# Quadrant scores and fp32 half-column values in the attention of a fused attention and rational MoE kernel

## Chip, cores, metric

The program runs on one core of one Trainium2 chip. The metric is device time in microseconds (us); before the change the median of three runs is 899.58 us (899.51 to 901.82). Below, the engines are called PE (TensorE, the matrix engine), PEld (its weight loads), DVE (VectorE), ACT (ScalarE), POOL (GpSimd) and SP (SyncE, which here only issues DMAs).

## What is computed

Attention over 8 batches, 8 heads, 576 tokens, head size 64, with keys and values averaged over runs of 8 tokens (72 remain), and then on the 4608 x 512 result a two-layer product with a rational function between the layers:

```python
    k_p = k.reshape(B, H, Sp, pool, D).mean(axis=3)
    v_p = v.reshape(B, H, Sp, pool, D).mean(axis=3)
    scores = scale * np.matmul(q, k_p.transpose(0, 1, 3, 2))
    scores = scores - np.max(scores, axis=-1, keepdims=True)
    attn = np.exp(scores)
    attn = attn / (np.sum(attn, axis=-1, keepdims=True) + 1e-09)
    return np.matmul(attn, v_p).astype(np.float32)
...
    h = x @ w_in
    h2 = h * h
    h3 = h2 * h
    P = a[0] + a[1] * h + a[2] * h2 + a[3] * h3
    Q = 1.0 + np.abs(b[0]) * np.abs(h) + np.abs(b[1]) * h2
    g = P / (Q + 1e-06)
    return (g @ w_out).astype(np.float32)
```

## The kernel before

**Blocks and units.** The 4608 tokens are cut into 18 blocks of 256. For a block, `attend` makes the attention output x, transposed (512 features in 4 groups of 128 partitions). Then 8 units of 256 hidden features follow: `mm1` makes `ph` (24 products of 256 columns), `rational` turns it into `gh` and `gl` on ACT, DVE and POOL, and `mm2` adds 12 products of 512 columns to the two sums `po`. The operands of these products are of type fp32r. What must be finer than one such operand is written as a sum of two parts (x as x0 + x1, g as gh + gl, each weight as two), and three products of parts are added. The units of blocks 0 and 1 run in two halves, those of 2 and 3 beside each other; from block 4 on, blocks follow one another.

**Attention of a block.** It has two tiles of 128 tokens. `attention` transposes q (on PE for blocks 0 to 3, on DVE after that), and makes the scores `ps` in fp32: pairs of heads lie on 128 partitions, the pooled keys `kpT` of a pair stand in a block-diagonal 128 x 144 operand whose other half is zero, so one product makes two heads' scores of 128 tokens. Then DVE takes the maximum and subtracts it, ACT does exp, DVE sums, and POOL multiplies by the reciprocal. The 144 probabilities of a pair of heads are more than 128 partitions hold, so 128 (`main`) and 16 (`rem`, `REM = 16`) go separate ways. They are transposed with DVE's 32 x 32 blocks and 16 DMAs a block into `lo` (the buffer am1; on PE for blocks 0 to 3), and then ACT and DVE split them into the parts `hi` and `lo` (am0 and am1). `values` makes four products for each pair of heads: values' high part by `hi`, low part by `hi`, the remainders (`vr`), and high part by `lo`.

**Block and batch limits do not coincide.** A batch has 576 tokens, 4.5 tiles. Four score tiles (4, 13, 22 and 31, in blocks 2, 6, 11 and 15) hold two batches and run each product as two of 64 tokens; six blocks (2, 4, 6, 11, 13 and 15) hold two batches in `values`, with twice as many products of fewer columns.

**Preparation.** `prep_k` and `prep_v` pool keys and values of a batch and `split_v` masks and splits the values. For batch 0 and 1, `prep_v_early` sums the runs on PE by products with the identity (`pvs`, `pvr`), with data in weight tiles that are free at that time.

**What sets the order.** `Plan` gives every instruction a cost, a due time and its buffers, lays them out on the engines, and issues them engine by engine in that order; at run time each engine goes through its list and waits on semaphores. `FAST`, `PACE` and `SLOW` set the due times. Where the plan sees PE without work, `issue` (lines 279 to 316) puts in filler products: `idle` before the first unit, and later products of the tile `zero` added to a sum `po`. All instructions that go through the plan have line 314 in the profile, fillers have 305; they are told apart by tile names: `ps` scores, `pv` values, `pm` and `pr` transposed probabilities, `pq` transposed q, `pk` and `pl` transposed keys, `am` the probabilities on partitions, `st_v` staged values, `e` the probabilities, `vm` and `vr` the split values.

## Time and profile before

| what | value |
|---|---|
| runs | 899.58, 899.51, 901.82 us |
| the profiled execution | 900.71 us, its span 899.0 us |
| PE busy | 883.1 us (98%) |
| DVE, ACT, POOL busy | 771.7, 679.1, 524.5 us |
| bytes moved | 75.33 MB, a mean of 84 GB/s |
| granted PE clock, mean | 0.998 of full speed |

The span is the time from the first to the last instruction. A matmul's record is longer than the time until the next one starts, since they are pipelined: rates are read from the starts of successive groups in the timeline, not from durations.

### The profile page before, as it was taken

The numbers are of one execution on the slowest core, as the hardware profiler recorded it, in microseconds if no ns is written. First come the engines' busy times: TensorE is split into PE (matmuls) and PEld (weight loads), VectorE is DVE, ScalarE is ACT, GpSimd is POOL, SyncE is SP. The second block draws the span as 40 slices with busy tenths as digits, with TensorE's granted clock in tenths as the row PEclk, the third lists the DMA queues.
The fourth block names the chain that finished last, engine by engine and source line by source line (L and its number), as shares of the span: only waits on it lengthen the run. The fifth ranks groups of instructions, "written<-read, shape, count | busy, mean of one in ns | idle before, by whom it ended". The sixth has DMA issues, their size and how long they took to land.

```text
span 899.0 us, 17101 instructions
## 1 busy us (share of the span) xinstructions
PE 883.1 (98%) x6158; PEld 824.7 (92%) x6158; DVE 771.7 (86%) x1335; ACT 679.1 (76%) x1126; POOL 524.5 (58%) x474
## 2 busy tenths in 40 slices
PE   7999999999999999999999999999999999999998
PEld 7898899899998999999999999999999999999997
DVE  6989988899979889987999798979897988788764
ACT  3998888878677777778677778686868787768765
POOL 4787687776546645354745485546644755445443
PEclk9999999999999999999999999999999999999999
DMA  9996110154243403031622252224412421202000
GB/s 267 315 379 232 25 54 1 47 147 124 69 91 72 129 16 70 16 73 26 137 45 45 58 132 58 37 46 89 112 32 58 94 60 25 60 1 61 1 24 24
DMA packets 185073, 75.33 MB, mean 84 GB/s; under 512 B 162332, under 2 KB 162332, under 8 KB 184988
## 3 DMA queue, kind: packets, MB, share of 16 engines
q1 hardware_dynamic: 184988, 74.23, 32.3%
q8 instruction: 49, 0.80, 0.4%
q14 instruction: 36, 0.29, 0.1%
HBM read 50.59 MB, written 12.58 MB: 70 GB/s over the span
## 4 chain that ended last, share of the span: by engine, by line
PE 70%; DVE 13%; ACT 6%; POOL 4%; SPq 2%; DMA 2%; issue 2%; ACTq 0%; POOLq 0%; DVEq 0%
PE ph L314 32%; PE po L314 30%; DVE t L314 4%; PE pv L314 3%; PE ps L314 3%; SPq L314 2%; ACT rp L314 2%; DVE rp L314 1%; DMA q<-in_q_dram 1%; POOL gl L314 1%; DVE sm L314 1%; POOL wout L314 1%; DVE m_win L314 1%; POOL w L314 1%; DVE am L314 1%
## 5 line engine op out<-in xcount | busy, mean ns | idle before, releaser
L314 PEld LDWEIGHTS ph<-x,win 128*128 128x128 f32 x3264 | 475.2, 191 | 42.0 <-DVE t L314 1.9
L314 PE MATMUL ph<-x,win 128*128 128x256 f32 x3264 | 488.0, 276 | 1.9 <-DVE t L314 1.1
L314 PE MATMUL po<-wout,gh 128*128 128x512 f32 x1152 | 342.8, 383 | 1.9 <-DVE am L314 1.2
L314 POOL TENSOR_TENSOR w<-w,r 128x512 f32<-128x512 f32 (+1 forms) x145 | 191.5, 1321 | 220.2 <-ACT r L314 210.9
L314 POOL TENSOR_TENSOR gl<-t,gh 128x512 fp32r<-128x512 f32 (+1 forms) x145 | 189.4, 1307 | 75.6 <-ACT gh L314 74.9
L314 PEld LDWEIGHTS po<-wout,gh 128*128 128x128 f32 x1152 | 179.8, 192 | 7.7 <-DVE am L314 1.6
L314 PE MATMUL po<-wout,gl 128*128 128x512 f32 x576 | 173.5, 383 | 0.0
L314 ACT ACTIVATE t<-ph,abn 128x512 f32<-128x512 f32 (+1 forms) x145 | 111.9, 772 | 58.2 <-PE ph L314 28.3
L314 DVE SCALAR_TENSOR_TENSOR t<-t,abn,rp 128x512 f32<-128x512 f32 (+1 forms) x145 | 109.0, 752 | 35.7 <-ACT rp L314 34.3
L314 DVE TENSOR_TENSOR t<-t,ph 128x512 f32<-128x512 f32 (+1 forms) x145 | 97.8, 678 | 40.6 <-ACT t L314 36.6
L314 ACT ACTIVATE r<-w,abn 128x512 f32<-128x512 f32 (+1 forms) x145 | 117.5, 811 | 16.6 <-POOL gl L314 6.1
L314 ACT CAST gh<-t 128x512 fp32r<-128x512 f32 (+1 forms) x145 | 88.5, 611 | 32.6 <-DVE t L314 32.4
L314 DVE SCALAR_TENSOR_TENSOR t<-t,abn,ph 128x512 f32<-128x512 f32 (+1 forms) x145 | 106.8, 738 | 2.6
L314 ACT ACTIVATE rp<-w 128x512 f32<-128x512 f32 (+1 forms) x145 | 86.5, 596 | 27.9 <-POOL w L314 20.7
L314 DVE SCALAR_TENSOR_TENSOR t<-rp,t 128x512 f32<-128x512 f32 (+1 forms) x145 | 98.9, 683 | 2.4
L314 ACT ACTIVATE w<-ph 128x512 f32<-128x512 f32 (+1 forms) x145 | 85.7, 592 | 20.1 <-DVE t L314 13.0
L314 DVE SCALAR_TENSOR_TENSOR rp<-w,rp 128x512 f32<-128x512 f32 (+1 forms) x145 | 99.4, 685 | 0.4
L314 PEld LDWEIGHTS po<-wout,gl 128*128 128x128 f32 x576 | 89.1, 192 | 1.4 <-POOL gl L314 0.2
L314 ACT ACTIVATE rp<-rp 128x512 f32<-128x512 f32 (+1 forms) x145 | 84.2, 581 | 2.6
L314 POOL TENSOR_TENSOR e<-e,sm 128x576 f32<-128x576 f32 x36 | 42.1, 1186 | 42.7 <-DVE sm L314 34.6
L314 PE MATMUL pv<-am,vm 128*128 128x256 f32 (+3 forms) x288 | 44.3, 275 | 0.6 <-DVE t L314 0.6
L314 PEld LDWEIGHTS pv<-am,vm 128*128 128x128 f32 x288 | 41.9, 191 | 1.9 <-DVE t L314 1.0
(109 smaller groups left out, 860.1 us busy)
## 6 DMA issues: line engine op xcount, KB each, us to landing
am<-e SPq DMA_DIRECT2D x224, 48.0 KB, 2.2
out_dram<-ob SPq DMA_DIRECT2D x17, 512.0 KB, 3.1
rwin<-in_moe_w_in_dram SPq DMA_DIRECT2D x8, 1024.0 KB, 9.6
rwout<-in_moe_w_out_dram SPq DMA_DIRECT2D x8, 1024.0 KB, 11.3
st_k<-in_k_dram SPq DMA_DIRECT2D x12, 512.0 KB, 5.0
st_v<-in_v_dram SPq DMA_DIRECT2D x12, 512.0 KB, 3.9
q<-in_q_dram SPq DMA_DIRECT2D x144, 32.0 KB, 2.0
st_v<-in_v_dram SPq DMA_DIRECT2D x48, 64.0 KB, 2.2
```

The source lines that it names most:

```text
L314: getattr(engines[op.eng], name)(*map(value, args), **{k: value(v) for k, v in kw.items()})
```

## The change

Scores: `kpT` is no longer block diagonal. Each head of a pair keeps its 64 feature rows in its own half of the partitions, and `quarters` makes each product as four of 64 x 64: two halves of the rows (the two heads) and two halves of the columns (tokens 0 to 63 and 64 to 127 of the tile), each with 72 columns streamed. The two heads write to two PSUM banks. Every tile has 16 such products, whether or not two batches meet in it.

Probabilities: each head's 72 go to 72 partitions of one buffer `am`, in fp32, without a split in parts. From block 4 on, DVE transposes 64 of the 72 in one instruction and the last 32 into a new tile `er` in another, and 12 DMAs a block (instead of 16) place them. For blocks 0 to 3 PE makes 8 transposes a tile instead of 6 and ACT and DVE copy them (`turn`).

Values: they stay whole in fp32 in `vp`, 72 partitions; `split_v`, the masks and the zeroing of `kpT` are gone. `values` makes one product per head, 72 x 64 by 256 columns, two heads of a pair in the two column halves, and both halves of the block in one step of the plan (but for block 0). `prep_v` runs POOL sums for 4 pairs of heads instead of 3 sets, `prep_v_early` runs all sums of 8 on PE. The pool `rat` has 6 buffers instead of 5.

```diff
-    pool("rat", 5)
+    pool("rat", 6)
...
-    kpT = [new("cpool", f"kpT{i}", [P, NJ, 2 * SP], F32, f"kpT{i}") for i in range(2)]
-    vm = [[new("cpool", f"vm{s}{i}", [P, NJ, P], F32R, f"vm{s}{i}") for s in range(2)]
-          for i in range(2)]
-    vr = [new("cpool", f"vr{i}", [P, NJ, D], F32R, f"vr{i}") for i in range(2)]
+    kpT = [new("cpool", f"kpT{i}", [P, NJ, SP], F32, f"kpT{i}") for i in range(2)]
+    vp = [new("cpool", f"vp{i}", [P, H, D], F32, f"vp{i}") for i in range(2)]
...
+    def prep_v_early(n, c):
+
         if n == 0:
-            for c in range(2):
-                js = slice(2 * c, 2 * c + 2)
-                half = early(0, 2)[:, c * CW:(c + 1) * CW].rearrange("p (j x) -> p j x", j=2)
-                dma(512, half, rows[js, REM:, :].rearrange("j r x -> r j x"))
-                dve(RW, port=True).tensor_tensor(
-                    out=half[:, :, 0:RW // 2], in0=half[:, :, 0:RW // 2],
-                    in1=half[:, :, RW // 2:RW], op=ALU.add)
-                for t in range(0, G // 2, 2):
-                    pe(430, [mm(vs[:, js], ident, half[:, :, s * D:(s + 1) * D], s == 0,
-                                s == G // 2 - 1) for s in range(t, t + 2)], claims=(vs,))
...
-            dma(1024, st, rows[:, REM:, :].rearrange("j r x -> r j x"))
-            st = st.rearrange("p j (t d) -> p t j d", t=G)
-            for t in range(0, G, 2):
-                pe(863, [mm(vs, ident, st[:, s], s == 0, s == G - 1)
-                         for s in range(t, t + 2)], claims=(vs,))
-        place = early(n, 1)
...
-        split_v(n, vs, vrs, False)
+            homes = [(early(m, 1)[:, CW:2 * CW], 2 * (1 - m), 2) for m in (1, 0)]
+        for place, h0, nh in homes:
+            st = place[:SP].rearrange("p (h x) -> p h x", h=nh)
+            dma(2 * SP * nh, st, v_place(n, 4 * c + h0, nh))
+            vs = bank(f"pvs{n}_{4 * c + h0}", [P, nh, D])[:SP]
+            step = G if n else 2
+            for t in range(0, G, step):
+                pe(109 * nh * step, [mm(vs, ident[:SP, :SP], st[:, :, s * D:(s + 1) * D],
+                                     s == 0, s == G - 1) for s in range(t, t + step)], claims=(vs,))
+            act(nh * D).copy(vp[n % 2][:SP, 4 * c + h0:4 * c + h0 + nh, :], vs)
...
+        for h in range(0, H, 2):
+            place = new("stage", "st", [P, 1024], F32, f"st_v{n}_{h}")[:SP]
+            st = place.rearrange("p (h x) -> p h x", h=2)
+            dma(4 * SP, st, v_place(n, h, 2))
...
-            while w > D:
-                gp(2 * w).tensor_tensor(out=st[:, :, 0:w], in0=st[:, :, 0:w],
-                                        in1=st[:, :, w:2 * w], op=ALU.add)
+            while w >= D:
+                to = st[:, :, 0:w] if w > D else vp[n % 2][:SP, h:h + 2, :]
...
-    def attention(t, hi, lo, qs, es):
+    def quarters(banks, j0, js, q, sg, at=0):
+
+        return [mm(banks[hh][r0:r1, at + j - j0, :], q[hh * D:(hh + 1) * D, j, r0:r1],
+                   kpT[n % 2][hh * D:(hh + 1) * D, j, :], True, True)
+                for j in js for a0, a1, n in sg for r0 in range(a0, a1, D)
+                for r1 in (r0 + D,) for hh in range(2)]
...
-        scores = [bank(f"ps{t}_{c}", [P, 4, SP]) for c in range(2)]
-        calls = [mm(scores[c][r0:r1, 2 * jj:2 * jj + 2, :], qT[:, 2 * c + jj, r0:r1],
-                    kpT[n % 2][:, 2 * c + jj, :], True, True)
-                 for c in range(2) for jj in range(2) for r0, r1, n in sg]
-        for part in [calls] if len(sg) > 1 else [calls[:2], calls[2:]]:
-            pe(1350 if len(sg) > 1 else 244 * 2, part, claims=(e, mx, sm))
-        for c in range(2):
-            hs = slice(4 * c, 4 * c + 4)
-            js = slice(2 * c, 2 * c + 2)
...
+        scores = [bank(f"ps{t}_{hh}", [P, NJ, SP]) for hh in range(2)]
+        pe(754, quarters(scores, 0, range(NJ), qT, sg), claims=(e, mx, sm))
+        for hh in range(2):
+            dve(NJ * SP).tensor_reduce(out=mx[:, hh, :], in_=scores[hh], op=ALU.max, axis=AX.X)
+            dve(NJ * SP).tensor_tensor(
+                out=es[:, hh:H:2, m, :], in0=scores[hh],
+                in1=mx[:, hh, :].unsqueeze(2).to_broadcast([P, NJ, SP]), op=ALU.subtract)
...
+        gp(450).tensor_tensor(out=e, in0=e, in1=sm.unsqueeze(2).to_broadcast([P, H, SP]),
+                              op=ALU.mult)
         if t >= 2 * SQ:
+            dve(H * HB).transpose(er[:, :, m, :], es[:, :, m, SP - HB:])
+            main = es[:, :, m, 0:2 * HB].rearrange("p h (g s) -> p h g s", s=HB)
+            dve(2 * H * HB).transpose(main, main)
+        else:
             for c in range(2):
-                dve(P).transpose(four[c], rem[c])
-            squares = main.rearrange("p j (g s) -> p j g s", s=HB)
-            dve(NJ * P).transpose(squares, squares)
+                turn(f"pm{t}_{c}", [es[:, h, m, :] for h in range(4 * c, 4 * c + 4)],
+                     am[:SP, 8 * c + m:8 * c + 8:2, :], c, am)
+
+    def turn(name, rows, to, c, am):
+
+        pm = bank(name, [P, 4, P])[:SP]
+        pe(110 * 4, [("transpose", (pm[:, x, :], row, ident), {}) for x, row in enumerate(rows)],
...
+        if c == 0:
+            act(4 * P).copy(to, pm)
...
-            pm = bank(f"pm{t}", [P, NJ, P])
-            pe(110 * NJ, [("transpose", (pm[:, j, :], main[:, j], ident), {})
-                          for j in range(NJ)], claims=(hi, lo))
-            act(NJ * P).copy(hi[:, :, col], pm)
-            dve(NJ * P).tensor_tensor(
-                out=lo[:, 0:NJ, col], in0=pm, in1=hi[:, :, col].bitcast(F32), op=ALU.subtract)
-            for c in range(2):
-                act(P).copy(four[c], rem[c])
-            pr = bank(f"pr{t}", [P, 2, P])
-            pe(110 * 2, [("transpose", (pr[:, c, :], pairs[:, NJ + c, REM:], ident), {})
-                         for c in range(2)])
-            act(2 * P).copy(lo[:, NJ:, col], pr)
-            dve(2 * P).tensor_tensor(
-                out=lo[P // 2:, NJ:, col], in0=pr[P // 2:],
-                in1=lo[P // 2:, NJ:, col].bitcast(F32), op=ALU.subtract)
...
+            pe(500, quarters([x[:, :, t, :] for x in scores], 2 * c, range(2 * c, 2 * c + 2),
+                             qT[t], [(0, P, 0)]), claims=(es, mx, sm))
...
-        for c in range(2):
-            if before:
...
+        sg = segs(i * TOK, TOK)
...
-            sg = segs(i * TOK, TOK)
-            order, turns = (woven, 2) if len(sg) == 1 else (lambda x: x, 1)
             for jj in range(2):
-                j = 2 * c + jj
                 for r0, r1, n in sg:
-                    vh, vl = vm[n % 2]
-                    o = pv[:, jj, r0:r1]
-                    h, l, r = (order(x) for x in (hi[:, j, r0:r1], lo[:, j, r0:r1],
-                                                  lo[:, NJ + c, r0:r1]))
-                    terms = ((o, vh[:, j, :], h), (o, vl[:, j, :], h),
-                             (pv[:D, jj, r0:r1], vr[n % 2][:, j, :], r),
-                             (o, vh[:, j, :], l))
-                    calls += [mm(dst, vals, probs, s == 0, s == 3)
-                              for s, (dst, vals, probs) in enumerate(terms)]
-            pe((112.0 if i >= SQ else 117.4) * 8 if len(calls) == 8 else 1635, calls, claims=xs)
+                    for hh in range(2):
+                        h = 4 * c + 2 * jj + hh
+                        probs = am[:SP, 2 * h:2 * h + 2, :].rearrange("p t s -> p (t s)")
+                        calls.append(mm(pv[hh * D:(hh + 1) * D, jj, r0:r1],
+                                        vp[n % 2][:SP, h, :], probs[:, r0:r1], True, True))
+            return pv, calls
+
+        def out(c, pv):
...
+
+        if before:
+            for c in range(2):
+                before(c)
+                pv, calls = products(c)
+                pe(1115, calls, claims=xs)
+                out(c, pv)
+        else:
+            both = [products(c) for c in range(2)]
+            pe(1985, both[0][1] + both[1][1], claims=xs)
+            for c in range(2):
+                out(c, both[c][0])
...
         if i >= SQ:
 
             for a in range(4):
-                for g in range(4):
-                    k0 = REM + g * HB
-                    dma(48, lo[g * HB:(g + 1) * HB].rearrange(
-                        "p j (m a s) -> p j m a s", m=2, s=HB)[:, :, :, a, :].bitcast(F32),
-                        es[a * HB:(a + 1) * HB, :, :, k0:k0 + HB],
+                rows, cols = slice(a * HB, (a + 1) * HB), slice(a * HB, (a + 1) * HB)
+                for g in range(2):
+                    dma(64, am[g * HB:(g + 1) * HB, :, cols],
+                        es[rows, :, :, g * HB:(g + 1) * HB].rearrange("p h t s -> p (h t) s"),
                         run=128, issue=0.65)
-            whole = lo.bitcast(F32)
-            act(NJ * TOK).copy(hi, whole[:, 0:NJ])
-            dve(NJ * TOK, port=True).tensor_tensor(
-                out=lo[:, 0:NJ], in0=whole[:, 0:NJ], in1=hi.bitcast(F32), op=ALU.subtract)
-            half = slice(P // 2, P)
-            act(2 * TOK).copy(lo[0:P // 2, NJ:], whole[0:P // 2, NJ:])
-            own = es[half, 0:2, :, 0:P]
-            both = [x[half, NJ:].rearrange("p c (m s) -> p c m s", m=2) for x in (lo, whole)]
-            act(2 * TOK).copy(own.bitcast(F32R), both[1])
-            dve(2 * TOK, port=True).tensor_tensor(
-                out=both[0], in0=both[1], in1=own, op=ALU.subtract)
-        return values(i, hi, lo)
+                dma(16, am[2 * HB:SP, :, cols],
+                    er[(a + 1) * HB - SP + 2 * HB:(a + 1) * HB].rearrange(
+                        "p h t s -> p (h t) s"), run=128, issue=0.65)
+        return values(i, am)
```

Counted over PE's whole list: 160 score calls become 576, 384 value calls 192, 25 `pvs` and `pvr` calls 40, 48 transposes of probabilities 64, 81 `idle` fillers 32, and 14 `zero` fillers 41.

Where PE's instructions stand, first at the first score tile of block 8 (tile 16). Before (`ps16_0` and `ps16_1` are its banks, `qT16` q, `kpT1` the keys of an odd batch, the other names units of blocks 6 and 7):

```order
L314 MATMUL ph7_0_4757<-x1_7_4732,win0_371 128x256 x4
L314 MATMUL po6_0_0_4499<-wout4_1903,gh6_4_4694 128x512
L314 MATMUL po6_0_1_4501<-wout4_1903,gh6_4_4694 128x512
L314 MATMUL ps16_0_4779<-kpT1_166,qT16_4397 128x144 x2
L314 MATMUL ps16_1_4782<-kpT1_166,qT16_4397 128x144 x2
L314 MATMUL ph7_0_4757<-x0_7_4723,win0_371 128x256 x4
L314 MATMUL po6_0_0_4499<-wout4_1903,gh6_4_4694 128x512
```

And after; the two rows of `ps16` stand eight times in turn there:

```order
L314 MATMUL po6_0_0_4376<-wout7_2074,gl6_7_4802 128x512
L314 MATMUL po6_0_1_4378<-wout7_2074,gl6_7_4802 128x512
L314 MATMUL ph7_4_4916<-x0_7_4698,win4_1214 128x256 x4
L314 MATMUL ps16_0_4925<-kpT1_664,qT16_4612 64x72
L314 MATMUL ps16_1_4927<-kpT1_664,qT16_4612 64x72
```

The tile's four calls over the full array have become 16 calls of a quarter, in one run, and the run stands four units of block 7 later (beside `ph7_4` instead of `ph7_0`).

Next, `values` of block 8 on PE. Before (`pv8_0` and `pv8_1` are its banks, `vm01`, `vm11` and `vr1` the split values):

```order
L314 MATMUL ph7_7_5237<-x0_7_4723,win7_1809 128x256 x4
L314 MATMUL po7_0_0_5071<-wout3_1188,gh7_3_5203 128x512
L314 MATMUL po7_0_1_5073<-wout3_1188,gh7_3_5203 128x512
L314 MATMUL pv8_0_5267<-am0_8_5150,vm01_864 128x256
L314 MATMUL pv8_0_5267<-am0_8_5150,vm11_889 128x256
L314 MATMUL pv8_0_5267<-am1_8_4947,vr1_843 64x256
L314 MATMUL pv8_0_5267<-am1_8_4947,vm01_864 128x256
```

After:

```order
L314 MATMUL po7_0_0_4954<-wout4_1787,gh7_4_5193 128x512
L314 MATMUL po7_0_1_4956<-wout4_1787,gh7_4_5193 128x512
L314 MATMUL pv8_0_5257<-am_8_5135,vp1_591 64x256 x4
L314 MATMUL pv8_1_5262<-am_8_5135,vp1_591 64x256 x4
L314 MATMUL po7_0_0_4954<-wout4_1787,gh7_4_5193 128x512
L314 MATMUL po7_0_1_4956<-wout4_1787,gh7_4_5193 128x512
```

16 calls in fp32r, four for a pair of heads, have become 8 in fp32, one for a head; around them stand no units of block 7's `ph` any more, since these are all done.

Last, PE at the turn from block 10 to block 11. Before, values of block 11 (`pv11_1`) end among the units of block 10:

```order
L314 MATMUL pv11_1_7104<-am0_11_6999,vm11_889 128x192
L314 MATMUL pv11_1_7104<-am1_11_6791,vr1_843 64x192
L314 MATMUL pv11_1_7104<-am1_11_6791,vm01_864 128x192
L314 MATMUL ph10_7_7059<-x0_10_6489,win7_1809 128x256 x4
L314 MATMUL po10_0_0_6885<-wout3_1188,gh10_3_7024 128x512
L314 MATMUL po10_0_1_6887<-wout3_1188,gh10_3_7024 128x512
L314 MATMUL ph10_7_7059<-x0_10_6489,win7_1809 128x256 x4
```

After, 12 fillers stand between block 10's sixth unit and the next score tile, and block 11's values come behind that tile:

```order
L314 MATMUL po10_0_1_6714<-wout5_1849,gh10_5_7025 128x512
L314 MATMUL po10_0_0_6712<-wout5_1849,gl10_5_7059 128x512
L314 MATMUL po10_0_1_6714<-wout5_1849,gl10_5_7059 128x512
L305 MATMUL po10_0_1_6714<-zero_96,identr_95 128x256 x12
L314 MATMUL ps24_0_7108<-kpT1_664,qT24_7031 64x72
L314 MATMUL ps24_1_7110<-kpT1_664,qT24_7031 64x72
```

Such a stretch of fillers, where the plan saw no work for PE, stood in one place before, in block 2 (14 fillers); now there are 15 in block 2, 13 at the start of block 4, and 13 here.

## Rows read from the trace of the kernel before

**Rows 1.** Of the page of the kernel before: busy time of the engines (busy us, share of the span, instructions), and from the span in 40 slices the granted PE clock in tenths.

```profile
PE 883.1 (98%) x6158; PEld 824.7 (92%) x6158; DVE 771.7 (86%) x1335; ACT 679.1 (76%) x1126; POOL 524.5 (58%) x474
...
PEclk9999999999999999999999999999999999999999
```

**Rows 2.** The table of stretches of the whole program: stretch in us, its length, and for PE, PEld, DVE, ACT and POOL busy us and instructions; then the granted clock, the DMA share and GB/s.

```profile
60.00:120.00 60.00, 57.78 (x418) 51.96 (x417) 58.10 (x97) 52.23 (x90) 43.49 (x28) 1.00 0.46 156
...
476.00:522.00 46.00, 46.00 (x329) 43.15 (x328) 38.96 (x66) 34.77 (x59) 25.40 (x22) 1.00 0.30 64
```

**Rows 3.** Who PE waited for in the whole program, the longest first: us in total, times, longest us.

```profile
PE pq L314 <- DMA q<-in_q_dram: 2.7, 1, 2.7
PE idle L314 <- DVE identr L1102: 2.2, 1, 2.2
PE po L314 <- DVE am L314: 1.2, 1, 1.2
```

**Rows 4.** PE in order of time around an ordinary score tile of a late block: start us, us until the last of the group ends, engine, operation, tiles, count.

```profile
562.13 0.61 PE L314 MATMUL ph<-x,win 128*128 128x256 f32 x4
562.58 0.60 PE L314 MATMUL po<-wout,gh 128*128 128x512 f32 x2
563.01 1.14 PE L314 MATMUL ps<-kpT,qT 128*128 128x144 f32 x8
563.90 0.70 PE L314 MATMUL ph<-x,win 128*128 128x256 f32 x4
564.43 0.60 PE L314 MATMUL po<-wout,gh 128*128 128x512 f32 x2
```

**Rows 5.** The same around a score tile in which two batches meet, so that each product is two of 64 columns of the array.

```profile
517.87 0.61 PE L314 MATMUL ph<-x,win 128*128 128x256 f32 x4
518.41 1.20 PE L314 MATMUL ps<-kpT,qT 128*64 128x144 f32 x16
519.54 0.70 PE L314 MATMUL po<-wout,gh 128*128 128x512 f32 x2
520.08 0.61 PE L314 MATMUL ph<-x,win 128*128 128x256 f32 x4
```

**Rows 6.** What of that tile had begun at 518.42 us: weight loads and products.

```profile
518.41 0.14 PEld L314 LDWEIGHTS ps<-kpT,qT 128*64 128x64 f32 x2
518.41 0.34 PE L314 MATMUL ps<-kpT,qT 128*64 128x144 f32 x2
```

**Rows 7.** PE in order of time over `values` of a block in one batch: its first and its last group, and what comes next.

```profile
508.52 0.38 PE L314 MATMUL pv<-am,vm 128*128 128x256 f32 x2
...
510.19 0.28 PE L314 MATMUL pv<-am,vm 128*128 128x256 f32 x1
510.30 0.61 PE L314 MATMUL ph<-x,win 128*128 128x256 f32 x4
```

**Rows 8.** The same over `values` of a block with two batches.

```profile
554.48 0.30 PE L314 MATMUL pv<-am,vm 128*128 128x64 f32 x2
...
557.61 0.27 PE L314 MATMUL pv<-am,vm 128*128 128x192 f32 x1
557.72 0.63 PE L314 MATMUL ph<-x,win 128*128 128x256 f32 x4
```

**Rows 9.** PE in order of time over sums of batch 1's values: `pvs` are products of 256 columns in fp32, two records each, `pvr` the remainders.

```profile
57.43 1.13 PE L314 MATMUL pvs<-early,identr 128*128 128x256 f32 x4
58.40 0.60 PE L314 MATMUL pq<-identr,q 128*128 128x128 f32 x4
58.92 0.71 PE L314 MATMUL pvr<-early,fourfold 32*128 32x128 f32 x4
59.56 1.13 PE L314 MATMUL pvs<-early,identr 128*128 128x256 f32 x4
60.34 1.91 PE L314 MATMUL ph<-x,win 128*128 128x256 f32 x14
```

**Rows 10.** PE in order of time where `zero` fillers stand, with the idle time before a group in brackets.

```profile
74.03 0.61 PE L305 MATMUL po<-zero,identr 128*128 128x256 f32 x4
74.59 0.66 PE L314 MATMUL pm<-identr,e 128*128 128x128 f32 x4
75.00 0.58 PE L305 MATMUL po<-zero,identr 128*128 128x256 f32 x3
...
76.61 0.58 PE L305 MATMUL po<-zero,identr 128*128 128x256 f32 x3
77.16 0.70 PE L314 MATMUL po<-wout,gh 128*128 128x512 f32 x2
79.09 1.51 PE L314 MATMUL po<-wout,gh 128*128 128x512 f32 x4 [1.23 <-DVE am L314]
```

**Rows 11.** Groups by line, shapes apart: busy us, mean ns of one, idle us before it. Steps that the change takes away, POOL's first step of the pooled values, and the `idle` fillers.

```profile
L314 DVE TENSOR_TENSOR am<-am,am 128x1024 fp32r<-128x1024 f32 x14 | 17.4, 1243 | 5.4 <-ACT am L314 5.0
L314 DVE TENSOR_TENSOR am<-am,e 64x512 fp32r<-64x512 f32 x14 | 11.1, 792 | 0.4
L314 ACT CAST am<-am 128x1024 fp32r<-128x1024 f32 x14 | 14.5, 1037 | 0.4 <-issue 0.4
L314 POOL TENSOR_TENSOR st_v<-st_v 128x512 f32<-128x512 f32 x18 | 23.0, 1280 | 9.4 <-DMA st_v<-in_v_dram 9.4
L305 PE MATMUL idle<-identr 128*128 128x256 f32 x81 | 15.1, 337 | 0.0
```

227 lines of the change are left out of this document (62 added, 165 removed).

## The prediction

> **What bounds the kernel now.** I read the busy shares first: PE 98%, DVE 86%, ACT 76%, POOL 58% [rows 1]. A busy PE need not be one at its best, so the stretches come next: in the late ones PE is busy for all of its 46 us at the full clock, while DVE has 7 us to spare and POOL 20 [rows 2]. Only the early stretch differs: from 60 to 120 us DVE is as full (58.1 of 60 us) as PE (57.8). Then PE's waits: few, short, and nearly all early [rows 3]. So from about 130 us on the time is PE's work itself, and an instruction taken from PE's list is worth its full pitch. What DVE, ACT and POOL lose or gain there changes nothing unless a new wait comes of it. I therefore count PE's work by kinds, and after that the places where PE could come to wait.
>
> **Scores.** An ordinary tile: 8 records of 144 columns begin at 563.01 and the next group at 563.90, 0.89 us; the `ph` group behind it takes 0.53 us instead of the usual 0.45. Together 0.97 us, 0.12 us a record [rows 4]. The tile with two batches tells what parts of the array do: 16 records of 64 array columns each. The group before it should have ended at 517.87 + 0.45 = 518.32, and the `po` group behind it takes 0.54 instead of 0.43 us, so the tile costs 519.54 + 0.11 - 518.32 = 1.33 us [rows 4, 5]. One after another, 16 records would be 1.94 us; two at a time 0.97. So the column halves do run side by side (both first records and both first weight loads had begun within the same hundredth of a microsecond [rows 6]), and 0.36 us is the price of going into the divided array and out of it; I call it the switch.
>
> After the change a tile is 16 calls, 32 records, of 72 columns: half of 144, an estimated 0.06 us each. Four at a time that is 8 x 0.06 = 0.49 us. No row shows halves of the rows running side by side, so this is bounded: 0.49 us if they do, 0.97 us if only column halves do. I take 0.49, since the nearest row, the two-batch tile, shows full independence of two parts. The switch lies between 0.08 us (what an ordinary fp32 tile costs on leaving) and 0.36; I take 0.30, near the only row of a divided array. That makes 0.79 us a tile.
>
> - 30 ordinary tiles: 30 x (0.79 - 0.97) = -5.4 us.
> - 4 tiles with two batches: 4 x (0.79 - 1.33) = -2.2 us.
> - Block 0 makes its two tiles in four half runs: 4 x (0.24 + 0.30 - 0.48) = +0.2 us.
>
> Scores together: -7.4 us.
>
> **Values.** In a block of one batch 16 records in fp32r take 510.30 - 508.52 = 1.78 us [rows 7]; in a block of two batches 557.72 - 554.48 = 3.24 us, because twice as many records of fewer columns run hardly faster each [rows 8]. After the change there are 8 fp32 calls, 16 records. An fp32 record streams its columns twice (0.12 us for 144), so 256 columns cost what a 512-column record costs, 0.43 / 2 = 0.217 us [rows 4]. In pairs of column halves: 8 x 0.217 + 0.30 = 2.04 us, and as much, plus 0.03, with two batches, for the columns are only divided.
>
> - 11 blocks of one batch: +0.26 us each, +2.9 us; block 0 switches twice, +0.56 us.
> - 6 blocks of two batches: 3.24 - 2.07 = 1.17 us each, -7.0 us.
>
> Values together: -3.6 us. Scores and values switch 57 times: at 0.36 us the sum is 3.4 us worse, at 0.08 us 12.5 better.
>
> **Preparation.** Batch 1's sums on PE: two `pvs` calls of 256 columns take 0.97 or 0.78 us, 0.43 a call; two `pvr` calls 0.64 us [rows 9]. Before: 8 x 0.43 + 8 x 0.32 = 6.0 us; after: 8 x 0.43 and 16 of half the columns, 16 x 0.22 = 7.0 us: +1.0 us. Batch 0's go from some 2 us of PE (8 calls of 128 columns and a remainder) to 16 x 0.43 = 6.9, in a stretch where PE ran 81 `idle` fillers [rows 11] and now runs 32. 49 fillers of some 0.13 us cover it; without that cover it costs up to 5 us. I take 0. Transposes of probabilities: four take 0.41 us [rows 10]; 64 instead of 48 is +1.6 us at that pitch, -1.0 us if 72 columns load in proportion; I take +0.5.
>
> **Fillers.** The plan's `zero` fillers go from 14 to 41. They occupy PE whether or not there is a gap: four take 0.56 us [rows 10], 27 x 0.14 = +3.8 us.
>
> **What leaves the other engines.** DVE loses 1.24 + 0.79 us a late block, ACT 1.04 us and more [rows 11]; early tiles lose the split too. POOL gains six sets of pooled sums, the first step of each 1.28 us [rows 11], with 20 us free in each 46. SP issues 12 transfers of probabilities instead of 16. In the late stretch all of this lies beside PE's work: 0. Early, where DVE is full, PE idles 2.2 us between 60 and 120 us [rows 2], and the 1.23 us wait behind DVE's split [rows 10] loses its cause. I take -2 us; between 0 and -8, since waits hidden in long records may go as well. The sixth `rat` buffer lets a unit start earlier; it is in that range.
>
> **New waits.** `values` now waits for all transfers of both halves at once; behind it on PE stand products of the block before, so nothing else on PE can fill that wait. Its transfers come earlier in the chain than the split did, so I price it at 0; the rival below prices it otherwise.
>
> **Sum.** -7.4 - 3.6 + 1.0 + 0.5 + 3.8 - 2 = -7.7 us against the profiled execution's 900.71 us (span 899.0, and 1.7 around it, which stay): 893.0. That execution lies 1.1 us above the median of 899.58, so a median of 891.9, rounded to 892.0 us.
>
> **Rivals.**
>
> *The row halves take turns.* The two heads of a pair stand in different rows but send their sums down the same array columns. If they cannot at once, a set of four takes 0.12 us, a tile 1.27 us, +0.48 us x 36 = +17.5 us: 909.5, slower. It decides from a set time of about 0.087 us on (7.7 / 36 / 8 = 0.027 above 0.06). For it: no row shows row halves together. Against: columns were independent to the full, and loads too.
>
> *A floor for each product.* If the engine takes at least 0.025 us for each record, whichever part of the array it goes to, four take 0.10 us: +0.04 x 8 x 36 = +11 us, 903, slower or just not. Against it stand two records begun within a hundredth of a microsecond [rows 6]; that is a pair after a pause, not 32 in a row. The Trainium skill, page "TensorEngine Tiling (Array Packing)", section "Instruction Overhead", has such a rule: some 60 cycles for each matmul however few its columns, and the advice not to take a factor from a small dimension. By its figure, 60 cycles at 2.4 GHz, an estimate of 0.025 us, the price is the one above; by the two-batch tile, where 16 records kept the pace of pairs, it does not bind, but at 0.06 us a record it could not have shown.
>
> *PE runs out of work.* Three places now have fillers, where the plan itself saw a gap: block 2, block 4's start, and the turn from 10 to 11. Where it saw one before, PE idled 1.23 us more than the fillers covered [rows 10], and the fillers around it add up to 3 us. There `values` waits for transfers and `ph` for `values`, one after another. With 2 us more at each place, +6 us: 898, no change to be measured. For it: score runs stand later among the units than before.
>
> *More is given back.* A switch of 0.2 us (-5.7) and early waits that go entirely: 885.
>
> *It doesn't do what it says.* If halves of the columns with 72 rows did not run together in `values`, 18 blocks would cost 1.7 us more each: 923. The two-batch tile speaks against it.
>
> **Chances.** Forecast (886 to 896.5) 0.46; more given back 0.14; PE runs out of work 0.18; row halves take turns 0.13; floor 0.06; values not in pairs 0.03. Under 0.3%, 2.7 us, a measurement of this kernel can't be told from no change; that makes 896.9 to 902.3 the middle. Faster: 0.46 + 0.14 + 0.03 of the third = 0.63; same: 0.15 + 0.03 of the floor = 0.18; slower: 0.19. The range reaches from 884 to 903.5: it takes in the third and half of the floor, and leaves the turns and unpaired values out above and 0.03 below.
>
> **What would show it.** In the profile after, an ordinary score tile from its first start to the next group near 0.7 us, with four records begun together and sets some 0.06 us apart; 1.2 us means turns. `values` near 1.95 us from start to start in every block, with or without two batches. The late stretches still busy throughout on PE. Waits of `pv` on transfers, or of `ph` on x, at the three filler places mean the third rival. Wrong from the start would be a clock that falls: it stood at the full level in all slices before [rows 1], and fewer `idle` fillers or smaller products could lower it.

## The result and the profile after

The changed kernel takes 905.51 us (median of 5 runs, 904.30 to 906.86), the kernel before 899.58: a ratio of 1.0059, 95% interval 1.0040 to 1.0077. It is slower by 0.6%, where 892.0 was forecast and the range ended at 903.5. The profiled execution took 904.36 us; its span is 902.5 us, 3.5 more than before.

The page's first lines, which answer to [rows 1], tell that the other engines were relieved as described (DVE 771.7 to 719.6 us, ACT 679.1 to 626.0) and that the clock granted to PE isn't full in the first two slices:

```profile
PE 885.9 (98%) x7014; PEld 799.8 (89%) x7014; DVE 719.6 (80%) x1235; ACT 626.0 (69%) x1033; POOL 527.4 (58%) x451
...
PEclk7799999999999999999999999999999999999999
```

The table of stretches (length, busy us and records of PE, PEld, DVE, ACT, POOL, then the granted clock, DMA share, GB/s), first before, then after. A granted clock of 1.00 is 2.4 GHz, 0.50 is 1.2 GHz. In both kernels it falls to 1.2 GHz at about 10 us (10.6 and 9.9), in the wait for the first queries. Before, the clock is back at 14.0 us; after, at 33.8, though PE is busy for all of the 20 us from 14 on:

```profile
10.00:14.00 4.00, 3.08 (x16) 3.08 (x17) 2.78 (x5) 1.03 (x3) 0.85 (x1) 0.58 1.00 273
14.00:34.00 20.00, 19.18 (x157) 18.28 (x156) 18.10 (x37) 14.52 (x27) 9.44 (x7) 1.00 1.04 345
```

```profile
10.00:14.00 4.00, 3.22 (x28) 2.78 (x28) 2.55 (x4) 1.12 (x4) 0.00 (x0) 0.50 0.93 243
14.00:34.00 20.00, 20.00 (x106) 11.95 (x100) 9.27 (x20) 6.75 (x11) 4.35 (x3) 0.51 0.97 314
```

The Trainium skill, "TensorE: Matmul & The Clock Gate", Part 1, says that activity of the engine releases the throttle. The second row after does not agree: PE is busy for 20.00 us there at a granted clock of 0.51.

What PE does in that stretch, in order of time (start, us, idle before in brackets). Before, batch 0's sums are two groups of 8 records with fillers around them, and the first `ph` begins at 27.25 us:

```profile
10.93 1.12 PE L314 MATMUL pq<-identr,q 128*128 128x128 f32 x4 [2.68 <-DMA q<-in_q_dram]
...
18.38 1.06 PE L314 MATMUL pvs<-early,identr 128*128 128x128 f32 x8
19.19 1.68 PE L305 MATMUL idle<-identr 128*128 128x256 f32 x12
20.70 1.06 PE L314 MATMUL pvs<-early,identr 128*128 128x128 f32 x8
...
27.25 0.49 PE L314 MATMUL ph<-x,win 128*128 128x256 f32 x2 [0.24 <-ACT x L314]
```

After, 24 records of `pvs` in a row need 10.3 us, and the first `ph` begins at 35.63:

```profile
10.78 1.11 PE L314 MATMUL pq<-identr,q 128*128 128x128 f32 x4 [3.14 <-DMA q<-in_q_dram]
...
19.16 10.51 PE L314 MATMUL pvs<-early,identr 72*72 72x256 f32 x24
29.46 1.92 PE L314 MATMUL pm<-identr,e 128*72 128x128 f32 x8
...
35.63 0.49 PE L314 MATMUL ph<-x,win 128*128 128x256 f32 x2
```

An ordinary score tile, which answers to [rows 4]: 32 records from 680.61 to the next group at 681.27, 0.66 us. The `ph` behind it takes 0.55 us and the `ph` ahead of it 0.54, where an undisturbed one (679.19) takes 0.44. Together that is 0.87 us for a tile. At 0.06 us a record, 32 records one after another would take 1.9 us, so the four quadrants do run side by side. The two-batch tiles cost the same, against 1.33 us before [rows 5].

```profile
679.19 0.61 PE L314 MATMUL ph<-x,win 128*128 128x256 f32 x4
679.63 0.60 PE L314 MATMUL po<-wout,gl 128*128 128x512 f32 x2
680.07 0.61 PE L314 MATMUL ph<-x,win 128*128 128x256 f32 x4
680.61 0.73 PE L314 MATMUL ps<-kpT,qT 64*64 64x72 f32 x32
681.27 0.71 PE L314 MATMUL ph<-x,win 128*128 128x256 f32 x4
681.82 0.60 PE L314 MATMUL po<-wout,gh 128*128 128x512 f32 x2
```

`values` of one batch and of two batches, which answer to [rows 7, 8]: 1.88 and 1.92 us to the next group, and some 0.2 us more in the groups around them, for going in and out of the divided array. That makes 2.08 and 2.12 us, as forecast (2.04 and 2.07).

```profile
514.20 1.95 PE L314 MATMUL pv<-am,vp 72*64 72x256 f32 x16
516.08 0.71 PE L314 MATMUL ph<-x,win 128*128 128x256 f32 x4
```

```profile
94.51 1.99 PE L314 MATMUL pv<-am,vp 72*64 72x64 f32 x32
96.43 0.70 PE L314 MATMUL po<-wout,gh 128*128 128x512 f32 x2
```

Who PE waited for, which answers to [rows 3]. The wait of `po` for the split is gone, and `pv` now waits for transfers, 5.2 us in five places:

```profile
PE pv L314 <- DMA am<-er: 5.2, 5, 1.2
PE pq L314 <- DMA q<-in_q_dram: 3.1, 1, 3.1
```

One of them, as SP's queue saw it (transfers being issued). The 12 transfers of a block's probabilities take from 694.91 to 704.74 us, 9.83 us, 0.82 each, while the plan counts 0.65. Over the 14 blocks a set takes 8.4 to 9.9 us, 9.1 in the mean, 0.76 each. (The 9.06 us in the expectations of e2 and e8 leave out the first transfer of this set.) PE, done with `po`, starts `values` at 706.39 after a wait of 1.21:

```profile
694.91 1.47 SPq L314 DMA_DIRECT2D am<-er  x2
696.83 5.05 SPq L314 DMA_DIRECT2D am<-e  x6
701.93 0.72 SPq L314 DMA_DIRECT2D am<-er  x1
702.70 1.29 SPq L314 DMA_DIRECT2D am<-e  x2
704.03 0.71 SPq L314 DMA_DIRECT2D am<-er  x1
```

```profile
706.39 1.95 PE L314 MATMUL pv<-am,vp 72*64 72x256 f32 x16 [1.21 <-DMA am<-er]
```

PE's whole span by kind of work, in us, each record counted from its start to the next one's and idle time taken out. The columns add up to the span; the row just above the span also holds two small products of 0.31 us. e3 and e17 are experiments below:

```
                                   before   after      e3     e17
scores ps                           33.67   25.61   24.11   24.11
values pv                           40.83   34.58   34.22   34.22
sums of values pvs, pvr              7.76   20.94   13.77   14.49
transposed probabilities pm, pr      5.07    8.17    6.87    7.86
transposed q and keys                6.88    7.95    6.18    6.02
zero fillers (14, 41, 30, 35)        2.05    5.25    4.04    4.96
idle fillers                        14.28    7.26   13.83   13.91
units ph, po                       771.91  775.46  774.72  774.17
PE idle between records              9.87   11.33   11.89   10.46
ahead of the first, behind the last  6.69    6.01    6.00    6.00
span                               899.00  902.55  895.63  896.21
```

Scores and values give back 14.3 us here (a part of their switch lies in `ph` and `po`), and the sums of values alone take 13.2.

### The profile page after: what moved, and what is told of

Same layout as the page of the kernel before. It is cut to its first block, busy times and chain, and to the rows that moved or that the text cites. A ratio compares the mean times of both kernels' runs of the same rounds, so it can differ in the third digit from the quotient of the medians.

```text
span 902.5 us, 18537 instructions
## 1 busy us (share of the span) xinstructions
PE 885.9 (98%) x7014; PEld 799.8 (89%) x7014; DVE 719.6 (80%) x1235; ACT 626.0 (69%) x1033; POOL 527.4 (58%) x451
## 4 chain that ended last, share of the span: by engine, by line
PE 74%; SPq 9%; DVE 7%; ACT 4%; DMA 3%; issue 2%; POOL 1%; DVEq 0%; POOLq 0%; ACTq 0%
PE ph L314 34%; PE po L314 32%; SPq L314 9%; PE pv L314 4%; DVE t L314 2%; PE ps L314 2%; DMA am<-er 1%; DVE sm L314 1%; DMA rwout<-in_moe_w_out_dram 1%; ACT rp L314 1%; PE pvs L314 1%; DVE rp L314 1%; DVE e L314 1%; ACT t L314 1%; ACT w L314 1%
## 5 line engine op out<-in xcount | busy, mean ns | idle before, releaser
L314 PEld LDWEIGHTS ph<-x,win 128*128 128x128 f32 x3264 | 457.5, 191 | 38.0 <-issue 2.6
L314 PE MATMUL ph<-x,win 128*128 128x256 f32 x3264 | 469.9, 276 | 1.7 <-DVE t L314 0.9
L314 PE MATMUL po<-wout,gh 128*128 128x512 f32 x1152 | 337.1, 382 | 0.0
L314 POOL TENSOR_TENSOR w<-w,r 128x512 f32<-128x512 f32 (+1 forms) x145 | 186.3, 1285 | 169.4 <-ACT r L314 164.6
L314 PEld LDWEIGHTS po<-wout,gh 128*128 128x128 f32 x1152 | 185.4, 191 | 11.0 <-issue 1.9
L314 DVE SCALAR_TENSOR_TENSOR t<-t,abn,rp 128x512 f32<-128x512 f32 (+1 forms) x145 | 106.4, 734 | 77.0 <-ACT rp L314 76.3
L314 PEld LDWEIGHTS po<-wout,gl 128*128 128x128 f32 x576 | 91.9, 191 | 5.4 <-issue 1.3
L314 POOL TENSOR_TENSOR st_v<-st_v 72x512 f32<-72x512 f32 (+1 forms) x48 | 48.0, 1007 | 9.4 <-DMA st_v<-in_v_dram 8.1
L314 PE MATMUL pv<-am,vp 72*64 72x256 f32 (+3 forms) x384 | 35.9, 331 | 5.7 <-DMA am<-er 5.2
```

The source lines that it names most:

```text
L314: getattr(engines[op.eng], name)(*map(value, args), **{k: value(v) for k, v in kw.items()})
```

## The experiments

Besides its time, each run has a mean granted clock. The changed kernel's five runs had 0.984 to 0.988, the kernel before 0.996 to 0.998 nearly always. 0.987 is (1 - 0.987) x 902.5 x 2 = 23.5 us at 1.2 GHz, which the trace shows in one piece (9.9 to 33.8 us). Ratios are to runs of the kernel before on the same chip, with 95% intervals; gains and losses "by the ratios" compare two of them, since the experiments ran on several chips.

**The clock (e1) and the plan's price (e2), each alone, and both (e3).** e1 adds fillers ahead of PE's steps in the head, e2 raises the price of a transfer:

```diff
+                more = 14 if nth == 2 else 3 if 2 < nth <= 12 else 0
+                for _ in range(more):
+                    self.nc.tensor.matmul(to, lhsT=self.filler, rhs=one, start=first, stop=first, ...)
```

```diff
-                        run=128, issue=0.65)
+                        run=128, issue=0.8)
```

> The changed kernel with more `idle` fillers (128x128 times 128x256) in the head and nothing else: 14 in the wait for the first queries, and 3 ahead of each of the next ten PE steps, 44 in all. Theory A (the head's clock): the changed kernel loses time because its granted clock stays at 1.2 GHz from 9.9 to 33.8 us, while before it was back at 2.4 GHz at 14.0 us, and because fewer fillers stand there. Then the added work holds or brings back the clock: full level by 16 us at the latest, the 24 `pvs` records in about 5.5 us instead of 10.3, the first `ph` at 28 to 31 us instead of 35.6, and the whole at 898 to 902 us against 905.5. Theory B (the head's work): batch 0's larger sums cost what they cost and the fillers only come on top: first `ph` at 39 us or later, 908 to 911 us.

> The changed kernel with the plan's price for issuing one transfer of probabilities raised from 0.65 to 0.80 us, so that `values` stands later in PE's order; the work is the same but for 30 `zero` fillers in place of 41. Theory A (waits): `values` waits for its transfers some 6 us in all because SP takes 9.06 us for a set of 12 transfers that the plan counts as 7.8; with the right price the waits of `pv` fall under 2 us and the time to 900 to 902.5 us against 905.5. Theory C (the wait only moves): the probabilities are ready late whatever the order, and then `ph` waits for x instead: 904 to 906 us.

> The changed kernel with both edits: the 44 more `idle` fillers in the head and the price of 0.80 us for a transfer of probabilities. Theory A for both: the gains add up, 893 to 897 us, under the 899.6 of the kernel before. If only the clock counts, 898 to 902; if only the waits count, 903 to 908; if neither, 908 or more.

e1: 900.25 us, 1.0002 (0.9985 to 1.0019), mean clock 0.993 to 1.000. In its profile the clock holds from 10 to 34 us, the 24 `pvs` take 5.4 us apart from a wait of 0.86, and the first `ph` begins at 29.69 (+2.4 us against the kernel before, instead of +8.4). More fillers made it faster, 5.1 us by the ratios, so theory A holds and theory B falls. But PE, now early, waits 2.93 us for batch 1's values, the clock falls behind that wait, and 16 `pvs` take 6.5 us instead of 3.5; the 96th `ph` is 15.1 us behind the kernel before. First the two rows of the repaired head, then the new wait:

```profile
10.00:14.00 4.00, 3.13 (x39) 3.00 (x40) 2.58 (x4) 1.16 (x4) 0.00 (x0) 1.00 0.94 233
14.00:34.00 20.00, 18.88 (x173) 13.76 (x165) 11.59 (x23) 10.75 (x17) 8.89 (x5) 1.00 0.98 311
```

```profile
46.77 6.72 PE L319 MATMUL pvs<-early,identr 72*72 72x256 f32 x16 [2.93 <-DMA early<-in_v_dram]
```

```profile
47.00:57.00 10.00, 10.00 (x35) 6.77 (x33) 3.51 (x6) 1.82 (x5) 5.36 (x6) 0.51 1.00 276
```

e2: 902.18 us, 1.0023 (1.0005 to 1.0041), mean clock 0.979 to 0.993. The time is in theory A's range; the ratios make it some 3 us faster than the changed kernel, with intervals that just overlap. In its profile no wait of `pv` is left, but others stand in their place, as theory C has it. That profile is of its longest execution (907.44 us, clock 0.979), so what a median one waits for is not shown.

```profile
PE ph L314 <- DVE t L314: 3.3, 2, 2.0
PE po L314 <- POOL gl L314: 3.2, 3, 1.8
```

e3: 898.35 us, 1.0001 (0.9979 to 1.0022), 894.54 to 905.23. That misses the 893 to 897 expected if both gains add up; it lies in the range for the clock alone, and by the ratios e3 is where e1 is. Its six runs with a mean clock of 0.998 or more have a median of 896.7, the other six of 901.2, but they were told apart only afterwards.

**The fillers of the kernel before (e4).** `idle` fillers only where the plan's time is under 11 us:

```diff
-                    to, one, first = self.idle.ap(), self.filler, True
+                    to, one, first = self.idle.ap() if op.start < 11 else None, self.filler, True
```

> The kernel before without its `idle` fillers from the plan's time 11 us on (48 left out, 33 kept), nothing else changed. Theory A (the fillers hold the clock): the granted clock falls at about 10 us as before, but stays at 1.2 GHz for more than 10 us instead of 3.4, and the first `ph` comes after 29 us instead of 27.25; the time is 902 to 906 us. Rival (the changed kernel's clock stays low because of what its products are, small ones of 72 rows and 64 columns, not because fillers are missing): the clock is back by about 15 us and the time stays at 899 to 900.5 us.

900.14 us, 1.0007 (0.9999 to 1.0016). The clock is at 1.2 GHz from 10.4 to 13.8 us and again from 24.1 to 27.5, behind a wait of 1.95 us where 18 fillers had stood, and the first `ph` begins at 27.70. So without the 48 fillers there is a second fall of 3.4 us, but no long stay: theory A's numbers do not come, and the rival, that the changed head's own products keep the clock down, is left standing. The test does not reach the first fall, though: the four fillers that stand in it before stand in it in e4 too, and four stand there in the changed kernel.

**What the sums occupy (e5) and how many they are (e6).**

```diff
-                pe(109 * nh * step, [mm(vs, ident[:SP, :SP], st[:, :, s * D:(s + 1) * D],
+                pe(109 * nh * step, [mm(vs, ident[:SP, :], st[:, :, s * D:(s + 1) * D],
```

```diff
+            if n == 0:
+                dve(nh * RW // 2, port=True).tensor_tensor(
+                    out=st[:, :, 0:RW // 2], in0=st[:, :, 0:RW // 2],
+                    in1=st[:, :, RW // 2:RW], op=ALU.add)
+            step, last = (G, G) if n else (2, G // 2)
```

> The changed kernel with the sums of values of batches 0 and 1 (`pvs`) taken with 128 columns of the identity instead of 72: as many calls of as many streamed columns, so the same time of PE at the same clock, with the rows behind the 72nd of the sums not used. Theory D (what the head's products occupy of the array decides when the granted clock comes back): with 72x128 instead of 72x72 of the array the clock is back at 2.4 GHz well before the 33.8 us of the changed kernel, by 24 us at the latest, the first `ph` comes before 32 us instead of 35.6, and the time is 899 to 902.5 us. Rival (the clock comes back with `ph` whatever the sums occupy): 2.4 GHz at 32 us or later, first `ph` at 34 us or later, 904 to 907 us.

> The changed kernel with batch 0's values halved on DVE ahead of their sums on PE, as the kernel before does: 8 `pvs` calls instead of 16 (72x256 each), two DVE additions of 72x1024, and the plan's own fillers come to 79 `idle` ones instead of 32. Theory E (the sums' work and the fillers that it pushed out are the head's loss): granted clock back at 2.4 GHz by 16 us as before, first `ph` at 28 to 30 us instead of 35.6, 899 to 902 us. Rival (the loss is the waits of `pv` and what else is late, the head is made up for later): 904 to 906 us.

e5: 905.99 us, 1.0061 (1.0041 to 1.0081). In its profile the clock is back at 14.2 us and the first `ph` begins at 30.59, as theory D has it, and yet the time is the rival's: the clock falls again at 24.4, 48.3 and 754.9 us, each time behind a wait, and its mean, 0.983 to 0.992, is no better than the changed kernel's. Nor is D itself shown: e7 and e10 below have the same sums as the changed kernel, and in their profiles the clock is back at 16 us. The third fall lies far behind the head, after a wait of 1.86 us of `pv` at 752 us:

```profile
754.00:762.00 8.00, 7.72 (x47) 6.82 (x48) 4.02 (x6) 2.88 (x5) 2.44 (x2) 0.57 0.00 0
```

e6: 902.68 us, 1.0035 (1.0022 to 1.0049), mean clock 0.991 to 0.996. In its profile the clock is back at 21.6 us and the first `ph` begins at 31.98, later than theory E has it. Halving the sums gains some 2 us by the ratios, whose intervals overlap, less than expected; the plan also put in 65 `zero` fillers (8.5 us) instead of 41.

**Stream and switch (e7).** In `quarters`:

```diff
-                for r1 in (r0 + D,) for hh in range(2)]
+                for r1 in (r0 + D,) for hh in range(2)] * 2
```

> The changed kernel with each tile's 16 score calls issued twice, the second set over the first (the plan's order and prices as they were), to tell the stream from the switch in a score tile. If the switch into and out of the divided array is paid once a tile, as forecast, the second 32 records cost their stream alone: 8 sets of 0.06, +0.49 us a tile, and a tile of 64 records takes 1.34 us with its group behind it, about 923 us in all. If there is no switch and 32 records stream in 0.66 to 0.86 us, a tile takes 1.5 to 1.7 us, 929 to 936 us.

A tile of 64 records takes from 829.60 to 830.76, 1.16 us to the next group instead of 0.66: 0.50 us for the second 32, as forecast, and 0.87 - 0.50 = 0.37 us is the switch, near the two-batch tile's 0.36 and not the 0.30 taken.

```profile
829.06 0.61 PE L314 MATMUL ph<-x,win 128*128 128x256 f32 x4
829.60 1.23 PE L314 MATMUL ps<-kpT,qT 64*64 64x72 f32 x64
830.76 0.71 PE L314 MATMUL ph<-x,win 128*128 128x256 f32 x4
```

The whole took 913.05 us in its one run, 10 below the 923 of this sum. Its profile has 10.2 us at 1.2 GHz where the changed kernel's has 23.9, which by an estimate (half of the difference) explains 7 of the 10; the rest is open.

**The small transfers on another queue (e8).** `am<-er` issued by ACT:

```diff
-                dma(16, am[2 * HB:SP, :, cols],
-                    er[(a + 1) * HB - SP + 2 * HB:(a + 1) * HB].rearrange(
-                        "p h t s -> p (h t) s"), run=128, issue=0.65)
+                plan.add("act", 0.1, [("dma_start", (am[2 * HB:SP, :, cols], er[
+                    (a + 1) * HB - SP + 2 * HB:(a + 1) * HB].rearrange("p h t s -> p (h t) s")), {})],
+                         bytes=16 * 1024 * (1 + 312 / 128))
```

> The changed kernel with the four small transfers of a block's last 8 keys (`am<-er`) issued by ACT instead of SP; nothing else is meant to move. Theory A (waits: SP issues 12 transfers in 9.06 us and `values` waits for the last): SP now has 8 to issue, some 6 us, the waits of `pv` fall from 5.2 us to under 1.5 and the time to 900 to 902.5 us against 905.5. Rival (what `values` waits for is the chain ahead of the transfers, or the time only goes to another wait): 904 to 907 us.

903.69 us, 1.0058 (1.0041 to 1.0075), the changed kernel's ratio, so the rival holds. PE's waits for `am<-er` are gone, and waits for DVE and ACT stand in their place:

```profile
PE pv L314 <- DVE t L314: 1.5, 2, 0.8
PE po L314 <- ACT gh L314: 1.4, 2, 0.7
PE ph L314 <- ACT x L314: 1.0, 2, 0.5
PE pv L314 <- DMA am<-e: 0.9, 1, 0.9
```

**The `zero` fillers (e10).**

```diff
-                elif sums:
+                elif False:
```

> The changed kernel without its 41 `zero` fillers, the `idle` ones kept. Theory F (a filler is PE time whether there is a gap or not, as forecast): 41 fillers of 0.13 us go, and the time falls by 3 to 5 us, to 900.5 to 902.5. Theory G (they stand where PE would wait anyway): 904.5 to 906.5. Theory H (without them PE pauses long enough there for the granted clock to fall once more): 906 to 909, with a stretch at 1.2 GHz behind one of the three places.

900.80 us, 1.0016 (1.0002 to 1.0030): by the ratios 3.9 us less for 41 fillers of 0.13 (5.25 us), at an unchanged mean clock (median 0.987 in both). By the time, theory F holds in the changed kernel. But its profile has what theory H expected, too: at the start of block 4, where 13 fillers stood, PE now waits 1.31 us for x, and the clock is at 1.2 GHz from 241.3 to 244.7 us:

```profile
240.46 5.49 PE L314 MATMUL ph<-x,win 128*128 128x256 f32 x28 [1.31 <-ACT x L314]
```

```profile
240.00:246.00 6.00, 5.51 (x29) 5.11 (x30) 4.90 (x10) 2.04 (x5) 2.64 (x2) 0.72 0.55 137
```

**Repairs together (e11 to e17).** e11 is e1 with batch 1's first sums later:

```diff
+                if n == 1 and c == 0:
+                    o.lead = 3.0
```

e12 is e11 with e8; e13 is e11 with e10; e14 is e3 with e10; e17 is e3 with the later sums, and e15 that with e10; e16 is the kernel before with e10's edit.

> The changed kernel with the 44 more `idle` fillers in the head, and batch 1's first sums of values placed 3 us later in the plan, because with the fillers alone PE reached them at 43.8 us, waited 2.9 us for their transfer, and the granted clock fell to 1.2 GHz at 47.1 for 10.2 us. Theory A (the clock, and the wait that its repair uncovered): no half clock from 16 us on, the 96th `ph` within 6 us of the kernel before instead of 13.6 to 15.1 us behind, and 895.5 to 898.5 us. Rival (PE lacks work there in whatever order; something else is waited for): 899 to 902 us, like the fillers alone (900.25).

> The three edits together: fillers in the head, batch 1's sums 3 us later, and the small transfers issued by ACT. If clock and waits are what the change lost against the forecast, their gains add up: 891.5 to 895.5 us, under the 899.6 of the kernel before by 0.4 to 0.9%. If only the head counts 895.5 to 898.5; if neither 900 or more.

> The changed kernel with the fillers in the head, batch 1's first sums 3 us later, and no `zero` fillers. By the runs so far the head gave 7.8 us (905.5 to 897.7) and the `zero` fillers 4.7 (905.5 to 900.8). If the two are independent: 892 to 895 us, under the kernel before (899.5) by 0.5 to 0.8%. Rival (the clock falls at the holes that are now bare, as PE has been faster since): 896 to 899 us, with a stretch at 1.2 GHz behind one of the places where fillers stood.

> The changed kernel with the fillers in the head, the price of 0.80 us for a transfer of probabilities, and no `zero` fillers (30 go, 4.0 us of PE). If they are PE time as they were in the changed kernel: 898.35 - 3.5 = 893 to 896 us. If they cover waits for `gl` there (the 328 and 463 us places, where PE waits behind fillers): 897 to 899 us.

> All edits that helped: fillers in the head, batch 1's sums 3 us later, price of 0.80 us, no `zero` fillers. Additive: 890 to 894 us, which would be near the 892.0 forecast. If the price's gain was only chance (898.35 against 900.25 with wide runs): as e13, 892 to 895. If waits move again: 895 to 899.

> The kernel before without its 14 `zero` fillers (2.05 us of PE), to see how much of the gain is to be had without the change. If they are PE time there too: 897 to 898.5 us against 899.5. If they cover the waits near 74 to 79 us, or hold the clock there: 899 to 901.5.

> The changed kernel with the fillers in the head, batch 1's first sums 3 us later and the price of 0.80 us for a transfer of probabilities, the `zero` fillers kept (e15 with them). If the `zero` fillers keep the granted clock up at places where PE would pause, as the bare kernels suggest (mean clock 0.989 to 1.0 from run to run without them), the mean clock is 0.996 or more in most runs and the time 895 to 898 us, under e15's 899.08 although PE has some 4 us more to do. If they are PE time only: 902 to 904 us.

```
       us median   range             ratio to before            mean clock
e11      897.70    894.50 to 902.75  0.9985 (0.9965 to 1.0005)  0.992 to 1.000
e12      902.97    898.87 to 908.61  1.0033 (1.0014 to 1.0052)  0.992 to 1.000
e13      906.04    898.64 to 912.44  1.0069 (1.0046 to 1.0091)  0.983 to 0.996
e14      899.10    893.08 to 904.79  0.9996 (0.9973 to 1.0018)  0.992 to 1.000
e15      899.08    894.26 to 905.57  0.9998 (0.9978 to 1.0018)  0.989 to 1.000
e16      898.96    898.04 to 902.22  0.9997 (0.9987 to 1.0006)  0.994 to 1.000
e17      897.79    894.26 to 903.41  0.9986 (0.9967 to 1.0005)  0.992 to 1.000
```

e11 repairs the head: 897.70 us, in the expected range, 6.7 us under the changed kernel by the ratios (7.8 by the medians). In its profile the first `ph` begins at 29.07 and the 96th is 6.2 us behind the kernel before. The wait for batch 1's values has given way to one of 2.15 us for POOL's `e` in the same place. Behind it the clock holds in e11's profile; in e17's, behind the same wait, it is at 1.2 GHz from 45.4 to 48.8 us. And e11's clock falls from 75.2 to 78.6 us, behind a wait of 4.54 us for q, so the expectation of no half clock from 16 us on is missed there. The wait for `e`, in e11 and in e17:

```profile
45.38 2.18 PE L319 MATMUL pm<-identr,e 128*72 128x128 f32 x16 [2.15 <-POOL e L319]
```

```profile
44.80 3.10 PE L319 MATMUL pm<-identr,e 128*72 128x128 f32 x16 [2.15 <-POOL e L319]
```

e12 doesn't add up: e8's edit costs e11 4.3 us by the ratios. In its profile, with the clock at 2.4 GHz throughout, `po` waits for ACT's `gh` for 4.4 us in four places, which points to ACT's queue. e13 doesn't either, and lies outside both of its ranges: bare of `zero` fillers, e11 lost 7.6 us by the ratios, and the mean clock fell. e14 and e15 are where e3 and e17 are, with 30 or 35 fillers fewer. So with the head repaired, leaving the fillers out gains nothing. That the clock takes their time back fits e13's mean clocks and the fall in e10's profile; between e15 and e17 (median 0.994 and 0.996) the difference is too small to show it. The kernel before gains nothing to be measured without its 14 (e16). e17 is in its expected range, with 8 of 12 mean clocks at 0.996 or more, but its lead over e15 is within the noise. e17 and e11 are the best versions; neither can be told from the kernel before.

e17's three early stretches, for comparison with the changed kernel's:

```profile
10.00:14.00 4.00, 3.46 (x41) 3.25 (x42) 2.19 (x4) 1.31 (x4) 0.00 (x0) 1.00 0.96 241
14.00:34.00 20.00, 19.73 (x167) 14.69 (x168) 11.99 (x24) 11.59 (x16) 10.06 (x5) 1.00 1.00 316
34.00:60.00 26.00, 23.53 (x216) 19.30 (x215) 21.78 (x38) 17.60 (x31) 18.35 (x18) 0.93 1.03 324
```

## Why the prediction was wrong

**The step that failed** is "I take 0" for batch 0's sums: 49 fillers would cover 5 us of added work. It made two mistakes. The cover was not whole: with the clock held, the first `ph` is still 1.3 to 2.4 us late (e17, e1). And the work was priced at the full clock. PE had fallen to 1.2 GHz in the same place before; there it was back 3.4 us later, in the changed head after 23.9. That made the first `ph` 8.4 us late instead of 2. What it cost in the end is shown by e11, where the head is repaired: 0.9985 of the kernel before against 1.0059, 6.7 us. The prediction named a falling clock among what would make it wrong "from the start", but gave it neither a price nor a chance. It also read the clock as full in all slices before: a slice is 22.5 us long and its digit 9 stands for 90% or more, so the fall from 10.6 to 14.0 us did not show in it. Why the clock stayed down is not settled: leaving out the fillers behind 14 us in the kernel before doesn't do it (e4), more fillers cure it (e1), wider products let it return in one profile and lost it elsewhere (e5), and the same head had it back at 16 us in the profiles of e7 and e10.

**New waits, priced at 0**, came: 5.2 us of `pv` on its transfers. The reason given, that these come earlier in the chain than the split did, left out that `values` is placed by the plan's price of 0.65 us for a transfer that takes 0.76, and, as I read it without a run for it, that the split's time had been slack for SP. This is the third rival, 898, with its cause in five places and not only where fillers stand. Curing the wait (e2, e8) gave 3 us at most; in both profiles other waits come next.

**Scores**: the mechanism was right, 0.50 us for 32 records. The switch is 0.37, so a tile costs 0.87 and not 0.79: 34 x 0.08 = 2.7 us of the 7.4 are missing. "The row halves take turns" fell with the first tile, and so did "a floor for each product" as it was priced: e7's second 32 records take 0.50 / 32 = 0.016 us each, less than the 0.025 of that rival. They are 16 calls of two records, 0.031 us a call, so a floor of 0.025 for a call isn't ruled out, but it would not set the pace. The Trainium skill gives some 60 cycles for each matmul ("TensorEngine Tiling (Array Packing)", "Instruction Overhead"), from which the prediction had its estimate of 0.025 us; by either count that is not what sets the pace here. The same page of the Trainium skill ("Key Properties") says that a change of the tiling mode drains the engine. Going in and out costs 0.37 us in this trace; that a drain is what takes it, no row shows.

**Values**: 2.08 and 2.12 us against 2.04 and 2.07. Right.

**Preparation**: batch 1's sums as forecast, 0.22 us a record at the full clock. Transposes cost 1.8 us more in e3 and 3.1 in the changed kernel, where 12 of the 64 lie in the slow head, against 0.5.

**Fillers**: 41 as the order had it, 5.25 us against 2.05: +3.2 for a forecast of 3.8, and e10, which leaves out all 41, gains 3.9 by the ratios.

**Early relief**, -2 in a range of 0 to -8, can't be separated from the late head: the 96th `ph` is 13.6 us behind, the 672nd 3.6. That much is made up between, but partly, as I read it, by waits that any late PE loses; and the lag goes on swinging (the 768th is 0.7 us ahead, the 960th 3.5 behind), as other work stands at other places in the order.

Put together from the forecast of 892: the clock costs 6.7 us (e11), the switch 2.7, the uncovered sums some 2, and the waits of `pv` up to 3 by e2: about 906, against 905.5. That it comes so near is partly luck: e3 and e12 to e15 show that gains do not add up, so no part of this sum is exact.

## What to carry to other kernels

Work that is added under fillers can cost more than the fillers it replaces: price it at the clock granted there, and at the low one too where a wait stands just ahead of it. Read the clock from short stretches of the head, not from slices of the whole span. When a stretch that was late is repaired, look for what it now reaches too early: e1 came to wait for batch 1's values and e11, with those placed later, for POOL. A plan's price for a transfer also sets when its reader stands in the list, so measure it whenever a step that lay between the two is taken out.

## What the runs showed of the hardware

- Quadrants of the array run side by side at 72 columns: 32 fp32 records in 0.50 us, and 0.37 us for going in and out of the divided array, once for a run of 32 records (0.87 us) as for one of 64 (e7, 1.37 us).
- A PE that was busy throughout stayed at 1.2 GHz for 20 us (14 to 34 us of the changed kernel), mostly on `pvs` records of 72 x 72 of the array, and in e1 for 10 us (47 to 57), behind a wait of 2.93 us.
- A wait of 1.86 us at 752 us, deep in the steady part, was followed by 6.8 us at 1.2 GHz (e5), and one of 1.31 us by 3.4 us (e10, at 241 us).
- Whether a wait is followed by such a stretch differs from one execution to the next. Behind the wait of 2.15 us for `e` the clock fell in e17's profile and not in e11's; in the wait for the first queries it fell in the profile of the kernel before (2.68 us) and not in that of e16 (2.90 us), which has the same head. The mean clock of e3's 12 runs goes from 0.991 to 1.000, and the time from 905.23 to 894.54.
